# A later Q block ahead of the first Wo, and weight loads limited to two or three under way, in a transformer block on one core

## The chip, the cores and the metric

The kernel runs on one core of a Trainium2 chip. The metric is the device time of one execution in microseconds (us), as the median of several runs. The engines are TensorE (PE; its weight loads are listed as PEld), VectorE (DVE), ScalarE (ACT), GpSimd (POOL) and SyncE (SP), which issues every DMA of this kernel.

## The reference

One pre-norm transformer block over 2048 tokens of width 1024, in bf16, with 32 heads of 32 and an FFN width of 3584:

```python
def _A_ref(x, wqkv, wo):
    qkv = (x @ wqkv).reshape(B, S, 3, H, Dh) -> q, k, v   # H = 32, Dh = 32
    p = softmax(q @ k.T * Dh ** -0.5)                     # full attention, no mask
    return concat_heads(p @ v) @ wo
def _B_ref(x, w1, b1, w2, b2):
    return gelu(x @ w1 + b1) @ w2 + b2                    # tanh form of gelu
h   = x + _A_ref(layernorm(x), wqkv, wo)
out = h + _B_ref(layernorm(h), w1, b1, w2, b2)
```

The block above is cut and put in short form; `_layernorm` has no weights, and `B_x` is not used.

## The kernel before

The program is first recorded as a graph of tasks and then put into an order for each engine by a planner written in the kernel (`Graph.schedule`). Each task has an engine, a list of instructions, a planned duration and a priority; dependencies come from the buffers that it reads and writes (`Graph.add`), also where two buffers overlap in SBUF. The planner walks through planned time and, for each engine, picks among the ready tasks the one with the lowest priority number and, among equals, the one recorded first. For TensorE `pick_pe` chooses: scores (`qk`) always first, then the products with V (`pv`) and the row sums (`den`) when enough rounds wait, and otherwise the background (`bg`): projections, Wo and FFN. The order is then fixed: every engine runs its own list, and semaphore waits are put where a task depends on another engine. SyncE's DMAs go round 24 semaphores ("lanes"), and a DMA waits for the one before it on its lane. Planned DMA time counts 280 GB/s.

Attention is cut into jobs `(qb, g)`: 256 queries (`qb` from 0 to 7) and a group of 4 heads (`g` from 0 to 7). A job has 8 rounds of 256 keys; a round is 8 score matmuls (L796, four heads side by side), two exps of 128x1024 on ScalarE (L807), then 8 matmuls with V (L833), and row sums (L862) over sums made on VectorE (L848). When a job ends, VectorE normalises it into `OT` (L893).

The stages are these. At the start x is normalised, transposed into `xnT` (four blocks of 512 tokens) and K, V and Q for group 0 are computed while the first jobs run. Then for g from 1 to 7 `rest_of_projections(g)` computes K of group g, part of V, and Q of the first 512 tokens, beside the jobs of `qb` 0 and 1 (and of `qb` 2 for g in `EXTRA`). Q of the second 512 tokens is computed there for groups 0, 1 and 2 only. The normalised and transposed x of token blocks 1 to 3 is stored to DRAM (`xd`, shown as x_scratch), since the SBUF under `xnT` and the QKV weights (`Wall`) is used again by the FFN's buffers. `late_q(qc, half, gs)` later loads a block of x back into `xq`, loads the Q weights again in blocks of 256 columns, and computes the missing Q, which goes to DRAM (`qd`, shown as q_scratch) and comes back job by job in `load_q`.

After that come, for each 256 tokens `u`: `wo(u)` (attention output times Wo plus x, into `hch`), `ln2(u)` (layer norm; on all but the last `u` a DMA transpose into `hnT`), `ffn1(u)` (14 blocks of W1, bias on VectorE, gelu by tanh on ScalarE, L1014), and `ffn2(u, j)` (two column halves, 7 blocks of W2 each, two token tiles per half). They are background work beside the jobs of `qb = u + 3`, and the last of them (from `wo(7)` on) run alone at the end. Helper lines: L556 and L559 are background matmuls as four 32-column parts and as a whole, L562 those of the tail, L580 every plain DMA, L585 the DMA transpose.

Weights come from DRAM in blocks of 512 KB, into rings: four slots for W1 (`a_w1r`) and seven for W2 (`a_w2r`). Wo's two halves of 1 MB (`wov`) take two W1 slots each, and the weight blocks of `late_q` are also taken from the W1 ring. For the last `u` there are rings over the former K and V (`b_w1r`, `b_w2r`). A load waits until the slot's last reader is done. W1, W2 and Wo loads have priority 1, the transposes and Q loads -1, output stores 0. Where the recorded order matters most:

```python
    block_copies()
    late_q(1, 1, [g for g in range(2, G) if g not in EXTRA])
    wo(0)
    ln2(0)
    late_q(2, 0, range(G))
    late_q(3, 1, range(G))
    ffn1(0)
```

Of the kernel before, what the change touches and what calls it, by code (L numbers as in the profile page):

```python
# [10 lines left out]
E = mybir.EngineType  # L11

P = 128
BF = dt.bfloat16
F32 = dt.float32


# [43 lines left out]
class Graph:  # L61
# [47 lines left out]
    def schedule(self, pick_pe, pool, switch=0.104, dma_rate=280.0, dma_lat=2.1, dma_issue=0.06):  # L109
# [10 lines left out]
        events = []  # L120
        n = 0
        num = {t: i for i, t in enumerate(self.tasks)}

# [17 lines left out]
        while n < total:  # L141
# [5 lines left out]
            for e in self.ENGS:  # L147
                while free[e] <= now + 1e-9:
# [6 lines left out]
                    if e == E.PE:  # L155
                        t = pick_pe(rd, now, state, free_banks(now))
                    else:
                        t = min(rd, key=lambda x: (x.prio, num[x]))
                        if up and t.prio > 0:

                            for (rt, _, u) in up[:6]:
                                if u.prio < t.prio and rt < now + 0.6 * t.occ:
                                    t = None
                                    break
# [14 lines left out]
                    seqs[e].append(t)  # L179
                    if e == E.SP:  # L180
                        k = min(range(self.n_lanes), key=lambda i: lanes[i].done if lanes[i] else 0.0)
                        if lanes[k] is not None:
                            t.deps.add(lanes[k])
                            start = max(start, lanes[k].done)
                        lanes[k] = t
                        t.lane = k
                        free[e] = start + dma_issue
                        s0 = max(state["dma"], start + 0.9)
                        state["dma"] = s0 + t.bytes / dma_rate / 1e3
                        t.done = max(state["dma"], s0) + dma_lat - 0.9  # L190
                    else:
                        free[e] = start + t.occ
                        t.done = start + t.occ + t.lat
# [135 lines left out]
def build_kernel(nc, A_x, A_wqkv, A_wo, B_w1, B_b1, B_w2, B_b2, out):  # L329
# [6 lines left out]
    G = D // P  # L336
# [82 lines left out]

    xnT, B_xnTt = sb(ph0, "xnT", [P, 4, DC, 512], BF, 4, 4)  # L420
    k_hi = Area(B_KT[8 * (G - 2)].lo)
    Wall, B_W = [], []
    for k in range(6):
        h, b = sb(k_hi if k == 2 else ph0, "Wall%d" % k, [P, DC, 512], BF, 1, 4)
        Wall.append(h)
        B_W.append(b)
    assert k_hi.cur <= B_V[0].lo
# [228 lines left out]
    def tr_tile(tt, bank, evac, prio=0):  # L656
        tc, t4 = divmod(tt, 4)
        transposes(xb[:, tt % NXB, :], B_xb[tt % NXB], bank, xnT[:, tc, :, t4 * P:(t4 + 1) * P], B_xnTt[tc][t4], evac, prio)

    def proj(which, g, tc, bank, evac, direct=False):  # L660
# [4 lines left out]
        for dc in range(DC):  # L665
            mm(bank, Wall[blk][:, dc, c:c + P], xnT[:, tc, dc, :], dc == 0, dc == DC - 1,
               [B_W[blk][c // P]] + B_xnTt[tc], True, after=free if dc == 0 else ())
# [54 lines left out]
    def proj_v(tt, q, bank, evac, after=()):  # L722
# [3 lines left out]
        for k in range(2):  # L726
            tc, t4 = divmod(tt + k, 4)
            for dc in range(DC):
                mm(bank, xnT[:, tc, dc, t4 * P:(t4 + 1) * P], Wall[blk][:, dc, c:c + 256], dc == 0, dc == DC - 1,
                   B_W[blk][c // P:c // P + 2] + [B_xnTt[tc][t4]], True, cols=(256 * k, 256 * k + 256), after=after)  # L730
# [6 lines left out]
    def proj_v1(tt, g, n, bank, evac, c0=0, narrow=False, after=()):  # L737

        for k in range(n):
            tc, t4 = divmod(tt + k, 4)  # L740
            for dc in range(DC):
                mm(bank, xnT[:, tc, dc, t4 * P:(t4 + 1) * P], Wall[4][:, dc, P * g:P * g + P], dc == 0, dc == DC - 1,
                   [B_W[4][g], B_xnTt[tc][t4]], narrow, cols=(c0 + P * k, c0 + P * k + P), after=after)
# [11 lines left out]
    def proj_half(which, hc, bank, evac):  # L755
# [3 lines left out]
        for dc in range(DC):  # L759
            mm(bank, Wall[blk][:, dc, 0:P], xnT[:, tc, dc, 256 * h:256 * h + 256], dc == 0, dc == DC - 1,  # L760
               [B_W[blk][0]] + B_xnTt[tc][2 * h:2 * h + 2], True, cols=(0, 256))
# [256 lines left out]
    def ffn2(u, j, wide=False, W=None, banks=None):  # L1018
# [4 lines left out]
        for q in range(FC // 4):  # L1023
            s = W.next("w2", W.nw2)
            dma(W.w2[:, s, :, :], w2d[j, q], P * 4096, reads=[B_w2d[j][q]], writes=[W.B_w2[s]], prio=1)
            ws.append(s)
# [36 lines left out]
    def lead_norm(hc):  # L1063
# [6 lines left out]
        for tt in tts:  # L1070
            if tt < LEAD_PE:
                tr_tile(tt, slot(), "act" if tt in LEAD_ACT else "dve")
            else:
                tc, t4 = divmod(tt, 4)
                last_t[:] = [dma_transpose(xnT[:, tc, :, t4 * P:(t4 + 1) * P], xb[:, tt % NXB, :], P * 2048, [B_xb[tt % NXB]], [B_xnTt[tc][t4]], -4)]
            if tt + 8 < NT:
# [33 lines left out]
    lx = last_t or last_x[-1:]  # L1110
    for tc in range(1, 4):
        dma(xd[tc - 1], xnT[:, tc, :, :], P * 8192, reads=B_xnTt[tc], writes=[B_xd[tc - 1]], prio=1)
    rest_w(WK, 2 * P, 3 * P)
# [39 lines left out]
    for g in range(1, G):  # L1153
# [5 lines left out]
        if g in EXTRA:  # L1159
            attention(2, [g])  # L1160
    for g in range(1, 2):
        if g not in EXTRA:
            proj(0, g, 1, slot(), "dve")
    block_copies()
    late_q(1, 1, [g for g in range(2, G) if g not in EXTRA])
    wo(0)
    ln2(0)
    late_q(2, 0, range(G))
    late_q(3, 1, range(G))
# [147 lines left out]
```

## Time and profile before

| | us |
|---|---|
| median of 3 runs | 1081.65 (1079.47 to 1082.18) |
| the profiled execution | 1080.46 |
| its span, first to last instruction | 1078.7 |
| TensorE matmul busy | 1041.8 (97%) |
| ScalarE busy | 1012.8 (94%) |
| VectorE busy | 751.5 (70%) |
| exps (L807), 1024 of them, busy | 924.5 + 31.3 |
| mean granted TensorE clock | 0.994 |
| DMA | 196.37 MB, mean 182 GB/s |

The durations of all matmuls are modelled at their ends and overlap, so a busy TensorE is not a TensorE at its peak. An instruction's mean duration is longer than its share of a full engine: 1024-wide exps last 1.116 us each and overlap. The granted clock is the TensorE clock that the throttle let through. In the lists of a timeline the bracket at the end of a line is the idle time of the engine before it and what ended it; what is named there is the one that came last by the profile among several that were waited for.

### The profile page before, as it was taken

The numbers are of one execution on the slowest core, as the hardware profiler recorded it, in microseconds if no ns is written. First come the engines' busy times: TensorE is split into PE (matmuls) and PEld (weight loads), VectorE is DVE, ScalarE is ACT, GpSimd is POOL, SyncE is SP. The second block draws the span as 40 slices with busy tenths as digits, with TensorE's granted clock in tenths as the row PEclk, the third lists the DMA queues.
The fourth block names the chain that finished last, engine by engine and source line by source line (L and its number), as shares of the span: only waits on it lengthen the run. The fifth ranks groups of instructions, "written<-read, shape, count | busy, mean of one in ns | idle before, by whom it ended". The sixth has DMA issues, their size and how long they took to land.

```text
span 1078.7 us, 41723 instructions
## 1 busy us (share of the span) xinstructions
PE 1041.8 (97%) x18987; PEld 608.7 (56%) x19044; DVE 751.5 (70%) x1438; ACT 1012.8 (94%) x1116; POOL 43.4 (4%) x110
## 2 busy tenths in 40 slices
PE   8999999998899999999999999999999999899998
PEld 6566555554344754674475457447545744474483
DVE  8766666566586896698499669849966967596401
ACT  4999999999999999999999999999999999999650
POOL 4200000000010001001000100100010001000100
PEclk9999999999899999999999999999999999899999
DMA  8560544438474645744764574476466455866260
GB/s 233 151 184 21 154 137 119 139 119 296 157 188 134 206 172 181 251 167 154 260 221 168 188 247 165 149 258 221 158 210 233 178 192 206 241 230 238 91 242 20
DMA packets 136177, 196.37 MB, mean 182 GB/s; under 512 B 49216, under 2 KB 100288, under 8 KB 133184
## 3 DMA queue, kind: packets, MB, share of 16 engines
q1 hardware_dynamic: 136000, 193.70, 53.8%
q8 instruction: 149, 2.44, 0.9%
q14 instruction: 28, 0.23, 0.1%
HBM read 177.94 MB, written 27.26 MB: 190 GB/s over the span
## 4 chain that ended last, share of the span: by engine, by line
ACT 74%; PE 24%; DVE 2%; issue 1%; POOL 0%; POOLq 0%
ACT PT L807 67%; PE ps L559 6%; PE ps L562 5%; PE ps L556 5%; ACT uu L1014 4%; PE ps L796 3%; ACT PX L807 3%; PE ps L833 2%; PE ps L862 1%; PE ps L1055 1%; DVE PS L848 0%; PE ps L629 0%; ACT xnT L636 0%; DVE hch L957 0%; DVE st L608 0%
## 5 line engine op out<-in xcount | busy, mean ns | idle before, releaser
L807 ACT ACTIVATE PT<-ps 128x1024 bf16<-128x1024 f32 x992 | 924.5, 1116 | 7.4 <-PE ps L796 7.3
L848 DVE TENSOR_TENSOR PS<-PT 128x1024 bf16<-128x1024 bf16 x431 | 286.8, 686 | 125.8 <-ACT PT L807 65.1
L796 PE MATMUL ps<-QT,KT 32*128 32x256 bf16 x4096 | 205.0, 274 | 8.9 <-ACT PT L807 5.7
L833 PE MATMUL ps<-PT,V 128*32 128x256 bf16 x3968 | 175.7, 274 | 3.6 <-ACT PT L807 3.5
L796 PEld LDWEIGHTS ps<-QT,KT 32*128 32x128 bf16 x4096 | 61.0, 92 | 164.6 <-ACT PT L807 145.3
L862 PE MATMUL ps<-PS,ones 128*32 128x256 bf16 x1756 | 122.2, 274 | 3.0 <-DVE PS L848 2.7
L559 PE MATMUL ps<-hnT,a_w1r 128*128 128x256 bf16 x979 | 119.1, 273 | 1.7 <-DVE hch L1037 0.5
L833 PEld LDWEIGHTS ps<-PT,V 128*32 128x32 bf16 x3968 | 101.6, 97 | 33.4 <-ACT PT L807 6.3
L559 PEld LDWEIGHTS ps<-hnT,a_w1r 128*128 128x128 bf16 x979 | 90.1, 98 | 26.7 <-issue 15.7
L556 PE MATMUL ps<-a_w2r,gT 128*32 128x512 bf16 x1380 | 99.8, 381 | 0.4 <-DVE gT L1016 0.3
L559 PE MATMUL ps<-a_w2r,gT 128*128 128x512 bf16 x390 | 96.2, 380 | 2.8 <-issue 1.9
L556 PE MATMUL ps<-hnT,a_w1r 128*32 128x256 bf16 x2356 | 83.4, 276 | 1.4 <-DVE gT L992 1.0
L992 DVE TENSOR_TENSOR gT<-ps,b1f 128x512 bf16<-128x512 f32 x98 | 67.3, 687 | 14.5 <-PE ps L559 8.0
L1037 DVE SCALAR_TENSOR_TENSOR hch<-ps,hch 128x512 bf16<-128x512 f32 x32 | 22.0, 689 | 72.1 <-PE ps L562 47.1
L556 PEld LDWEIGHTS ps<-hnT,a_w1r 128*32 128x32 bf16 x2356 | 58.5, 97 | 15.2 <-issue 11.7
L559 PEld LDWEIGHTS ps<-a_w2r,gT 128*128 128x128 bf16 x411 | 35.3, 98 | 46.9 <-issue 12.5
L862 PEld LDWEIGHTS ps<-PS,ones 128*32 128x32 bf16 x1756 | 46.3, 96 | 25.1 <-DVE PS L848 8.8
L1014 ACT ACTIVATE uu<-uu 128x1024 bf16<-128x1024 bf16 x49 | 57.2, 1168 | 0.0
L559 PE MATMUL ps<-xnT,Wall 128*128 128x512 bf16 (+1 forms) x256 | 54.0, 344 | 2.4 <-issue 1.0
L556 PEld LDWEIGHTS ps<-a_w2r,gT 128*32 128x32 bf16 x1380 | 29.9, 96 | 25.7 <-issue 15.2
L613 POOL CAST mvb<-mv 128x2 bf16<-128x2 f32 (+1 forms) x25 | 5.1, 211 | 976.4 <-DVE mv L610 976.4
L878 DVE STREAM_TRANSPOSE OD<-ps 128x256 f32<-128x256 f32 x64 | 28.6, 447 | 11.5 <-PE ps L833 5.9
(91 smaller groups left out, 1018.4 us busy)
## 6 DMA issues: line engine op xcount, KB each, us to landing
a_w2r<-w_blocks SPq DMA_DIRECT2D x105, 512.0 KB, 5.6
a_w1r<-w_blocks SPq DMA_DIRECT2D x98, 512.0 KB, 3.7
wov<-wo_blocks SPq DMA_DIRECT2D x16, 1024.0 KB, 4.8
w_blocks<-in_B_w_dram SPq DMA_DIRECT2D x28, 512.0 KB, 4.0
b_w1r<-w_blocks SPq DMA_DIRECT2D x14, 512.0 KB, 4.1
a_w1r<-in_A_wqkv_dram SPq DMA_DIRECT2D x11, 512.0 KB, 5.2
Wall<-in_A_wqkv_dram SPq DMA_DIRECT2D x17, 256.0 KB, 4.5
xrb<-in_A_x_dram SPq DMA_DIRECT2D x16, 256.0 KB, 4.7
```

The lines of the kernel that those rows point to most:

```text
L556: fns.append(lambda p, j=j: p.matmul(psum[32 * j:32 * j + 32, bi(bank), c0:c1], lhsT[:, 32 * j:32 * j + 32], rhs, start=start, stop=stop, ...
L559: t.whole = lambda p: p.matmul(psum[:, bi(bank), c0:c1], lhsT, rhs, start=start, stop=stop, skip_group_check=True)
L562: t = pe(lambda p: p.matmul(psum[:, bi(bank), c0:c1], lhsT, rhs, start=start, stop=stop), occ, reads=reads, writes=[bb(bank)], mode="full" ...
L796: return p.matmul(psum[:, 2 * us[h // 2] + h % 2, 256 * i:256 * i + 256], KT[32 * h:32 * h + 32, g, k0:k0 + P], QT[32 * h:32 * h + 32, qs, :],
L807: act(lambda a, u=u, k=k: a.activation(PTs[s][:, k, :, :], psum[:, 2 * u:2 * u + 2, :], ACT.Exp, bias=0.0, scale=SCALE), 1024, reads=[B_ps ...
L833: fns.append(lambda p, i=i, h=h: p.matmul(psum[32 * h:32 * h + 32, bi(bank), 0:256], V[:, g, 2 * r + i, 32 * h:32 * h + 32], PTs[s][:, h / ...
L848: dve(lambda v: v.tensor_tensor(PS[:, n, :, :], pairs[:, :, 0:256], pairs[:, :, 256:512], ALU.add), c_dve(1024, 2), reads=B_PTs[s], writes ...
L862: fns.append(lambda p, h=h, rhs=rhs, i=i: p.matmul(psum[32 * h:32 * h + 32, bi(bank), 256:512], ones32[:, :], rhs, start=False, stop=last, ...
L878: t = dve(lambda v: v.transpose(OD[:, o, 1, :], psum[:, bi(bank), 256:512]), 0.36, reads=[self.B_O, self.B_D], writes=B_D, prio=-1)
L992: t = dve(lambda v: v.tensor_tensor(g[:, fc:fc + 2, :], psum[:, bi(bank), :].rearrange("p (f c) -> p f c", f=2), b1f[:, fc:fc + 2].unsquee ...
L1014: act(lambda a: a.activation(w, w, ACT.Tanh, bias=0.0, scale=KT2), 1024, reads=[B_uu[i]], writes=[B_uu[i]], prio=-1)
L1037: drop(dve(lambda v, hs=hs, bank=bank, half=half: v.scalar_tensor_tensor(hch[:, hs, c], psum[:, bi(bank), :], half, hch[:, hs, c], ALU.mul ...
```

## The change

The change has four parts.

1. The SBUF under `xnT` and `Wall` is laid out anew, so that the second block of x (`xnT1`) and the Q weights (`Wall0`, `Wall1`) lie under buffers that are needed late or not at once. Q of the second 512 tokens is then computed for groups 3 to 7 from `xnT1` and `Wall`, as it was for group 1 and 2. `late_q(1, ...)` is gone, and with it the store of that block of x. Other buffers lie elsewhere as a result: `hch` over `xnT1`, `xq` over `Wall4` and `xnT0`, the W1 ring over `xnT2`, `xnT3` and `Wall3`, the W2 ring over `Wall3`, `Wall5`, `Wall0` and `Wall1`.
2. `late_q(2, ...)` is recorded ahead of `wo(0)` and `ln2(0)`.
3. W2 loads get priority 2 and so yield to W1 and Wo loads.
4. Loads of 512 KB or more of priorities 1 and 2 are counted in units of 512 KB. The planner lets one go only when it makes at most three units (priority 1) or two (priority 2) under way, and adds a dependency on the completion of the load that has to be finished first. These loads are planned at 350 GB/s.

```diff
+BULK = {1: 3, 2: 2}
+UNIT = 1 << 19
...
+        def behind(t):
+            k = BULK[t.prio] - t.bytes // UNIT
+            for b in reversed(bulk):
+                k -= b.bytes // UNIT
+                if k < 0:
+                    return b
+            return None
...
-                        t = min(rd, key=lambda x: (x.prio, num[x]))
+                        go = rd
+                        if e == E.SP:
+                            go = []
+                            for x in rd:
+                                b = behind(x) if x.bytes >= UNIT and x.prio in BULK else None
+                                if b is None or b.done <= now + 1e-9:
+                                    go.append(x)
+                                else:
+                                    heapq.heappush(events, b.done)
+                            if not go:
+                                break
+                        t = min(go, key=lambda x: (x.prio, num[x]))
...
                     if e == E.SP:
+                        if t.bytes >= UNIT and t.prio in BULK:
+                            b = behind(t)
+                            if b is not None:
+                                t.deps.add(b)
+                            bulk.append(t)
...
-                        state["dma"] = s0 + t.bytes / dma_rate / 1e3
+                        state["dma"] = s0 + t.bytes / (350.0 if t.bytes >= UNIT and t.prio in BULK else dma_rate) / 1e3
...
-    xnT, B_xnTt = sb(ph0, "xnT", [P, 4, DC, 512], BF, 4, 4)
...
+    Wall[2], B_W[2] = sb(k_hi, "Wall2", [P, DC, 512], BF, 1, 4)
+    for kind, k in (("x", 1), ("W", 4), ("x", 0), ("x", 2), ("x", 3), ("W", 3), ("W", 5), ("W", 0), ("W", 1)):
+        h, b = sb(ph0, ("xnT%d" if kind == "x" else "Wall%d") % k, [P, DC, 512], BF, 1, 4)
...
-            dma(W.w2[:, s, :, :], w2d[j, q], P * 4096, reads=[B_w2d[j][q]], writes=[W.B_w2[s]], prio=1)
+            dma(W.w2[:, s, :, :], w2d[j, q], P * 4096, reads=[B_w2d[j][q]], writes=[W.B_w2[s]], prio=2)
...
-    for tc in range(1, 4):
-        dma(xd[tc - 1], xnT[:, tc, :, :], P * 8192, reads=B_xnTt[tc], writes=[B_xd[tc - 1]], prio=1)
+    for tc in range(2, 4):
+        dma(xd[tc - 1], xnT[tc][:, :, :], P * 8192, reads=B_xnTt[tc], writes=[B_xd[tc - 1]], prio=1)
...
-    for g in range(1, 2):
-        if g not in EXTRA:
-            proj(0, g, 1, slot(), "dve")
+    for g in range(3, G):
+        proj(0, g, 1, slot(), "dve")
     block_copies()
-    late_q(1, 1, [g for g in range(2, G) if g not in EXTRA])
+    late_q(2, 0, range(G))
     wo(0)
     ln2(0)
-    late_q(2, 0, range(G))
     late_q(3, 1, range(G))
```

More of the change, by code (lines that the diff above doesn't have):

```diff
@@ L121, in schedule @@
         n = 0
+        bulk = []
+        def behind(t):
[5 more added lines that the diff above has]
+            return None
         num = {t: i for i, t in enumerate(self.tasks)}
@@ L417, in build_kernel @@
     ffn = Area(top.cur)
-    xnT, B_xnTt = sb(ph0, "xnT", [P, 4, DC, 512], BF, 4, 4)
     k_hi = Area(B_KT[8 * (G - 2)].lo)
[L422 to L426, printed above, removed]
+    Wall, B_W = [None] * 6, [None] * 6
+    xnT, B_xnTt = [None] * 4, [None] * 4
+    Wall[2], B_W[2] = sb(k_hi, "Wall2", [P, DC, 512], BF, 1, 4)
+    for kind, k in (("x", 1), ("W", 4), ("x", 0), ("x", 2), ("x", 3), ("W", 3), ("W", 5), ("W", 0), ("W", 1)):
+        h, b = sb(ph0, ("xnT%d" if kind == "x" else "Wall%d") % k, [P, DC, 512], BF, 1, 4)
+        if kind == "x":
+            xnT[k], B_xnTt[k] = h, b
+        else:
+            Wall[k], B_W[k] = h, b
     assert k_hi.cur <= B_V[0].lo
@@ L657, in tr_tile @@
         tc, t4 = divmod(tt, 4)
-        transposes(xb[:, tt % NXB, :], B_xb[tt % NXB], bank, xnT[:, tc, :, t4 * P:(t4 + 1) * P], B_xnTt[tc][t4], evac, prio)
+        transposes(xb[:, tt % NXB, :], B_xb[tt % NXB], bank, xnT[tc][:, :, t4 * P:(t4 + 1) * P], B_xnTt[tc][t4], evac, prio)
     def proj(which, g, tc, bank, evac, direct=False):
@@ L665, in proj @@
         for dc in range(DC):
-            mm(bank, Wall[blk][:, dc, c:c + P], xnT[:, tc, dc, :], dc == 0, dc == DC - 1,
+            mm(bank, Wall[blk][:, dc, c:c + P], xnT[tc][:, dc, :], dc == 0, dc == DC - 1,
                [B_W[blk][c // P]] + B_xnTt[tc], True, after=free if dc == 0 else ())
@@ L728, in proj_v @@
             for dc in range(DC):
-                mm(bank, xnT[:, tc, dc, t4 * P:(t4 + 1) * P], Wall[blk][:, dc, c:c + 256], dc == 0, dc == DC - 1,
+                mm(bank, xnT[tc][:, dc, t4 * P:(t4 + 1) * P], Wall[blk][:, dc, c:c + 256], dc == 0, dc == DC - 1,
                    B_W[blk][c // P:c // P + 2] + [B_xnTt[tc][t4]], True, cols=(256 * k, 256 * k + 256), after=after)
@@ L741, in proj_v1 @@
             for dc in range(DC):
-                mm(bank, xnT[:, tc, dc, t4 * P:(t4 + 1) * P], Wall[4][:, dc, P * g:P * g + P], dc == 0, dc == DC - 1,
+                mm(bank, xnT[tc][:, dc, t4 * P:(t4 + 1) * P], Wall[4][:, dc, P * g:P * g + P], dc == 0, dc == DC - 1,
                    [B_W[4][g], B_xnTt[tc][t4]], narrow, cols=(c0 + P * k, c0 + P * k + P), after=after)
@@ L759, in proj_half @@
         for dc in range(DC):
-            mm(bank, Wall[blk][:, dc, 0:P], xnT[:, tc, dc, 256 * h:256 * h + 256], dc == 0, dc == DC - 1,
+            mm(bank, Wall[blk][:, dc, 0:P], xnT[tc][:, dc, 256 * h:256 * h + 256], dc == 0, dc == DC - 1,
                [B_W[blk][0]] + B_xnTt[tc][2 * h:2 * h + 2], True, cols=(0, 256))
@@ L1074, in lead_norm @@
                 tc, t4 = divmod(tt, 4)
-                last_t[:] = [dma_transpose(xnT[:, tc, :, t4 * P:(t4 + 1) * P], xb[:, tt % NXB, :], P * 2048, [B_xb[tt % NXB]], [B_xnTt[tc][t4]], -4)]
+                last_t[:] = [dma_transpose(xnT[tc][:, :, t4 * P:(t4 + 1) * P], xb[:, tt % NXB, :], P * 2048, [B_xb[tt % NXB]], [B_xnTt[tc][t4]], -4)]
             if tt + 8 < NT:
```

## The prediction

> **What bounds the kernel now.** I read the busy shares first, then the windows by engine, then ScalarE's own timeline for its gaps, then SyncE's timeline.
>
> ```profile
> PE 1041.8 (97%) x18987; PEld 608.7 (56%) x19044; DVE 751.5 (70%) x1438; ACT 1012.8 (94%) x1116; POOL 43.4 (4%) x110
> ACT  4999999999999999999999999999999999999650
> PEclk9999999999899999999999999999999999899999
> ```
>
> ScalarE (ACT) is full in 36 of 40 slices, and the clock row dips twice, near 290 and near 930 us. ScalarE's 1024 exps and 49 tanhs run back to back: the chain of waits has 178 exps in 163.48 us, 0.918 us each, so 1073 of them are 985.5 us. The first starts at 22.28 and the last ends at 980.76 + 31.43 = 1012.2. That leaves about 4.3 us of gaps, and ScalarE's timeline lists nearly all of them:
>
> ```profile
> 292.21 11.12 ACT L807 ACTIVATE PT<-ps 128x1024 bf16<-128x1024 f32 x12 [1.55 <-PE ps L796]
> 303.52 16.89 ACT L807 ACTIVATE PT<-ps 128x1024 bf16<-128x1024 f32 x18 [0.19 <-PE ps L796]
> 646.20 2.86 ACT L807 ACTIVATE PT<-ps 128x1024 bf16<-128x1024 f32 x3 [0.47 <-PE ps L796]
> 729.20 8.36 ACT L807 ACTIVATE PT<-ps 128x1024 bf16<-128x1024 f32 x9 [0.22 <-PE ps L796]
> 917.41 14.83 ACT L807 ACTIVATE PT<-ps 128x1024 bf16<-128x1024 f32 x16 [0.37 <-PE ps L796]
> 933.74 8.36 ACT L807 ACTIVATE PT<-ps 128x1024 bf16<-128x1024 f32 x9 [1.50 <-PE ps L796]
> ```
>
> The bracket is the idle time before the group: 1.74 us around 290 to 303, 1.87 us around 917 to 933, 0.69 us elsewhere. After 1012.2 comes a tail of 66.5 us of plain matmuls. So the change can win at most 4.3 us (0.4%) before the tail, and it has to win it in those places. The windows show why they are there (busy us of each engine in each stretch, then granted clock, DMA share, GB/s):
>
> ```profile
> 259.00:266.70 7.70, 5.00 (x105) 1.97 (x108) 4.03 (x7) 7.63 (x10) 0.00 (x0) 1.00 0.95 347
> 281.60:289.00 7.40, 4.37 (x80) 1.59 (x78) 4.26 (x11) 7.40 (x9) 0.00 (x0) 0.73 0.82 288
> 289.00:303.50 14.50, 14.31 (x227) 6.52 (x228) 9.95 (x20) 12.78 (x14) 2.23 (x4) 0.90 0.41 97
> 917.00:930.20 13.20, 9.09 (x182) 3.45 (x183) 7.24 (x13) 12.83 (x15) 0.00 (x0) 0.87 1.08 277
> 930.20:935.00 4.80, 4.54 (x100) 2.75 (x96) 1.07 (x3) 3.30 (x5) 0.00 (x0) 0.65 0.16 61
> ```
>
> Three times TensorE (first pair) runs out of background work (projections, Wo, FFN) and only serves attention. ScalarE stays full meanwhile. In the second and third stretch the granted clock then falls to 0.50 (in 2 us windows, 286 to 290 and 928 to 932), and ScalarE loses its time just afterwards, when background work is back and TensorE still runs at half clock. The first stretch is starved as long, but keeps its clock and costs nothing.
>
> **The change part by part.** Sums are against the profiled execution: 1080.46 us, its span of 1078.7 plus 1.76 around it. The median of the runs, 1081.65, lies 1.2 above it.
>
> *Q of the second 512 tokens from resident x.* Gone are one 1 MB store, one 1 MB load and three 512 KB weight loads (11 of that row become 8). The 5 x 8 matmuls stay, with the same 512 columns. The stretch 259 to 266.7 was the wait for that load of x (issued around 251 to 256) and its weight block; TensorE gets about 2.7 us of background time back there. ScalarE lost nothing in it: value 0.
>
> *The later Q block ahead of the first Wo.* At 281.6 TensorE had finished the old late Q, and wo(0) had to wait for attention head group 7: its OT is written at 288.14 + 0.41 and wo(0) starts at 289.02. late_q(2) stood behind wo(0) because its weight blocks take ring slots that Wo's weights hold. In the changed program's order it comes first: 64 matmuls x 0.22 us (24 in 5.3 us in the tail) = 14 us of TensorE work in front of a hole where 7.40 - 4.37 = 3.0 us are free. Counting the background matmuls between one round of scores and the next, the order of before has six rounds without any in this neighbourhood (two, then four in a row), the new one has one, and that is full of attention work. So I take the first clock drop as gone: -1.55 - 0.19 = -1.74. Two prices. wo(0) comes later by the 14 us of work; the background of the attention phase ends at 1004.2 (last ffn2(6,0) matmul) against the last exp at 1012.2, which is 8 us of cover, and the refilled 5.7 us go into it. If that cover were gone, each us would cost one. And the first block of late_q(2) can load only when the last V matmul has released the x under its ring slot; 16 projection matmuls (3 rounds, 5.5 us) stand in between, and such loads land in 5.2 us (median). Bound 0 to 1.5; I take 0.3, since the median just fits.
>
> *Buffers in another order.* The w2 ring now lies under weight blocks that the late Q projections still read, so its early loads wait for them; they are first read at 401, over 100 us later. The x rows for Wo (hch) wait for the last projection from the second x block; they land in 4.5 us, and late_q(2) covers them. 0 for both.
>
> *Two or three weight loads under way, w2 behind w1.* SyncE issues in order, so a wait for a load holds up everything queued behind it: Q loads (needed many rounds later), output stores, and the two DMA transposes of hnT that FFN1 needs. Before, the queue looked like this ahead of the last starved stretch:
>
> ```profile
> 904.46 2.96 SPq L580 DMA_DIRECT2D a_w1r<-w_blocks  x4
> 907.92 3.35 SPq L580 DMA_DIRECT2D a_w2r<-w_blocks  x4
> 911.31 3.60 SPq L585 DMA_TRANSPOSE hnT<-a_xb  x1
> 915.01 1.04 SPq L580 DMA_DIRECT2D b_w1r<-w_blocks  x1
> 916.09 0.43 SPq L580 DMA_DIRECT2D a_w2r<-w_blocks  x1
> 916.56 2.80 SPq L585 DMA_TRANSPOSE hnT<-a_xb  x1
> ```
>
> Ten blocks, 5.2 MB, are ahead of the second transpose; at the 390 GB/s of those windows that is 13 us, and the transposes' landing spreads from 2.7 to 8.9 us. With at most 1.5 MB under way the backlog is 4 us, so the transpose gains up to 6. But the order takes this back: before, half of ffn2(5,1) lay between the end of wo(6) (906.4) and the hole (918.3), 11.9 us of cover for layer norm and transposes. In the new order ffn2(5,1) is done first and three of the four tiles of wo(6) are the last background work. The chain behind them is exposed: 8.1 us from the last add to a_xb (907.32 to 915.45), about 1 for the add, 1.3 to issue and 2.8 to 6.8 to land, 13 to 17 us, against a hole of 11.9 before. The order shows six rounds without background there in both programs. So I keep the second drop: 0, with bounds -1.87 (no drop) and +1.9 (a longer stay at half clock, once more the same loss).
>
> Supply under the limit: a load lands in 3.9 us (median of a_w1r) and takes 0.35 to issue, so two under way bring a block every 2.1 us, three every 1.4. A pass of ffn2 over one token tile reads a block per four matmuls, 0.88 us of TensorE, about 1.5 us beside attention. Over the six later blocks two under way fall 3.6 us behind, unless the first lies ready that much earlier. Slots are released one by one in the pass before, some 10 us ahead, so I take 0; bound 3.6 for a pass. [...] In the tail the last b_w1r load is issued at 1010 for a stage that starts at 1027, and a_w2r and b_w2r over 20 us ahead: 0.
>
> Sum: 1080.46 - 1.74 + 0.3 = 1079.0 as a profiled execution, and 1.2 more as a median: **1080.2**.
>
> **The rivals.**
> *Both clock drops go* (0.2). For it: the transposes lose their backlog, and equally starved stretches have not always dropped the clock (259 to 266.7). Against it: six rounds without background in the new order. 1081.65 - 1.74 - 1.87 + 0.3 = 1078.3. [...]
> *Nothing is gained* (0.2). The drop at 290 comes elsewhere, for example where wo(0) waits for its second half of weights (1 MB, landing 4.6 to 10.2 us, loadable only when late_q(2) has left the slots). For it: two rounds near there have a single background matmul. 1081.65.
> *Slower: w2 starves ffn2* (0.1). Place: the first pass of ffn2 in the five stages u = 1 to 5, where w2 now yields to w1 and waits two deep. If the first block is ready less than 3.6 us ahead, TensorE, which runs in order, stops with the next scores behind the stopped matmul. Half the shortfall, 1.8 us less 0.3 in hand, five times is 7.5 us: 1080.2 + 7.5 = 1087.7. Against it: SyncE's loads never show as TensorE waits in the trace of before.
>
> **How the numbers follow.** The forecast, one drop gone and one kept, gets 0.5. The measurement tells about 0.3% (3.2 us) from no change; the three runs spread over 2.7. Faster by more needs less than 1078.4: half of the both-drops case and the lower end of the forecast, 0.17. Slower by more needs over 1084.9: the w2 case and a little, 0.11. Between them 0.72. The range goes from 1077.6 (both drops and the small gaps) to 1083.2 (no gain, and the 1.5 us of the first block).
>
> **What would show it.** Right: clock 1.00 from 259 to 303, no ScalarE gap over 0.3 us there, a hole without background just before ffn1(6) at some 910 to 925 with clock 0.50 behind it and 1.5 to 2 us of ScalarE gaps, the last exp at about 1010.7, the same tail of 66.5 us. Wrong: a full clock throughout (then both drops), a drop between 285 and 310 (no gain), or ScalarE gaps that repeat every 94 us at the start of ffn2 (starved w2).

## The result, and the profile after

The changed kernel takes 1090.44 us (median of 6 runs, 1087.05 to 1091.86), the kernel before 1080.82 us on the same chip (6 runs). The ratio is 1.0087, 95% interval 1.0069 to 1.0104: slower by 0.9%, where 1080.2 us was forecast, a change too small to measure. The profiled execution took 1091.77 us with a span of 1089.8, against 1080.46 and 1078.7.

The page of the changed kernel, the lines that answer to those of before (busy time and share by engine, the rows of slices, and the shares of the chain of waits):

```profile
PE 1052.4 (97%) x18834; PEld 607.8 (56%) x18834; DVE 749.7 (69%) x1438; ACT 1014.9 (93%) x1116; POOL 44.1 (4%) x110
ACT  4999999999999999999999999999999999899650
PEclk9999999999999999999999999999999999899899
ACT 50%; PE 31%; DMA 13%; DVE 5%; issue 1%; POOL 1%; SPq 1%; POOLq 0%; DVEq 0%
```

The first dip of the clock row, near 290 us, is gone, and there is a new one shortly before the tail. In the chain DMA has 13%; before, the same row had none:

```profile
ACT 74%; PE 24%; DVE 2%; issue 1%; POOL 0%; POOLq 0%
```

ScalarE's timeline of the changed kernel shows where it stood still; the bracket is the idle time ahead of a group:

```profile
450.50 1.02 ACT L840 ACTIVATE PT<-ps 128x1024 bf16<-128x1024 f32 x1 [0.58 <-PE ps L829]
486.91 29.61 ACT L840 ACTIVATE PT<-ps 128x1024 bf16<-128x1024 f32 x32 [0.95 <-PE ps L829]
517.42 26.73 ACT L840 ACTIVATE PT<-ps 128x1024 bf16<-128x1024 f32 x29 [0.90 <-PE ps L829]
...
668.39 4.69 ACT L840 ACTIVATE PT<-ps 128x1024 bf16<-128x1024 f32 x5 [0.99 <-PE ps L829]
...
811.41 14.93 ACT L840 ACTIVATE PT<-ps 128x1024 bf16<-128x1024 f32 x16 [0.85 <-PE ps L829]
...
935.95 1.94 ACT L840 ACTIVATE PT<-ps 128x1024 bf16<-128x1024 f32 x2 [2.27 <-PE ps L829]
939.10 9.27 ACT L840 ACTIVATE PT<-ps 128x1024 bf16<-128x1024 f32 x10 [1.21 <-PE ps L829]
...
1012.15 9.32 ACT L840 ACTIVATE PT<-ps 128x1024 bf16<-128x1024 f32 x10 [0.79 <-PE ps L829]
1024.71 0.39 ACT L915 ACTIVATE OD<-ps 128x256 f32<-128x256 f32 x1 [3.24 <-DVE OD L911]
```

All listed gaps up to the last exp make 11.56 us, against 4.30 before. To see what each came from one asks TensorE's timeline just ahead of it. TensorE waits of 0.15 us or longer that a DMA ended did not exist before. There are 11 now, 7.5 us in all: ten for weight loads (6.2 us) and one for the transpose into hnT. Four of them:

```profile
483.34 1.90 PE L592 MATMUL ps<-wov,OT 128*128 128x512 bf16 x8 [1.03 <-DMA wov<-wo_blocks]
516.00 1.04 PE L592 MATMUL ps<-a_w2r,gT 128*128 128x512 bf16 x4 [0.82 <-DMA a_w2r<-w_blocks]
809.65 0.61 PE L589 MATMUL ps<-a_w2r,gT 128*32 128x512 bf16 x8 [0.81 <-DMA a_w2r<-w_blocks]
933.88 1.47 PE L589 MATMUL ps<-hnT,a_w1r 128*32 128x256 bf16 x24 [1.36 <-DMA hnT<-a_xb]
```

ScalarE's gaps at 486.91, 517.42, 811.41 and 935.95 stand right behind them. The chain of waits around the second of these, and SyncE's timeline (issue time, time to issue, DMAs in a row) show the limit at work:

```profile
507.02 4.54 DMA a_w2r<-w_blocks
...
511.58 4.37 DMA a_w2r<-w_blocks
...
516.00 1.04 PE ps L592 x4
```

```profile
501.72 0.32 SPq L613 DMA_DIRECT2D a_w2r<-w_blocks  x1
503.51 0.32 SPq L613 DMA_DIRECT2D QT<-q_scratch  x1
503.87 0.43 SPq L613 DMA_DIRECT2D a_w2r<-w_blocks  x1
505.74 1.24 SPq L618 DMA_TRANSPOSE hnT<-a_xb  x1
507.02 1.24 SPq L613 DMA_DIRECT2D a_w2r<-w_blocks  x2
510.58 0.34 SPq L613 DMA_DIRECT2D out_dram<-hch  x1
511.58 4.71 SPq L613 DMA_DIRECT2D a_w2r<-w_blocks  x3
```

These are the seven W2 blocks of the second pass of ffn2 in this stage (the second column half). They go out over 14.6 us. Four of them, the one at 501.72 and the last three, start when an earlier load has just landed; the transpose of hnT stands in the same queue. TensorE reads the first four blocks between 510.69 and 515.18:

```profile
510.69 1.67 PE L592 MATMUL ps<-a_w2r,gT 128*128 128x512 bf16 x7 [0.17 <-DVE hch L1070]
...
512.63 1.47 PE L592 MATMUL ps<-a_w2r,gT 128*128 128x512 bf16 x6
...
514.36 0.82 PE L592 MATMUL ps<-a_w2r,gT 128*128 128x512 bf16 x3
```

The fifth, which it reads at 516.00, was issued at 511.58, when one that was issued at 507.02 had landed. In the kernel before, the seven blocks of the same pass went out within 6.1 us (509.71 to 515.84):

```profile
509.71 6.13 SPq L580 DMA_DIRECT2D a_w2r<-w_blocks  x7
```

Set against its first matmul, each block of a second pass was issued 7 to 11 us ahead in the kernel before (second trace, e9 below) and landed 1.8 us or more ahead. In the changed kernel the lead falls within each such pass from 7 to 9 us to about 4, and one block or more lands only as it is read. Up to the tail the blocks of the first passes are issued over 45 us ahead in both kernels.

The windows of the changed kernel (busy us of PE, PEld, DVE, ACT, POOL, then granted clock, DMA share, GB/s) give the clock:

```profile
281.60:289.00 7.40, 7.11 (x128) 3.35 (x118) 5.74 (x12) 7.40 (x9) 0.00 (x0) 1.00 0.75 244
921.00:928.00 7.00, 4.01 (x80) 1.64 (x72) 5.54 (x15) 6.74 (x8) 2.43 (x4) 0.78 1.02 239
928.00:940.00 12.00, 8.98 (x188) 4.84 (x188) 4.31 (x7) 8.44 (x9) 0.00 (x0) 0.70 0.66 178
1014.00:1020.00 6.00, 4.15 (x68) 1.21 (x68) 2.46 (x4) 6.00 (x8) 0.00 (x0) 0.75 0.01 3
```

The hole at 281.6 is filled and keeps its clock. The hole ahead of ffn1(6) is still there. Ahead of the tail the last background matmul ends 9.7 us before the last exp, 8.0 before the change, and the clock now drops there as well: the tail's first ScalarE step waits 3.24 us instead of 1.44, and the tail takes 68.3 us instead of 66.5.

The whole difference of the spans, by term:

| term | us |
|---|---|
| first clock drop gone (1.55 + 0.19) | -1.7 |
| nine ScalarE gaps behind waits for loads of W1, W2, Wo | +5.5 |
| gaps around ffn1(6), 3.82 instead of 1.87 | +1.9 |
| other listed gaps, 2.2 instead of 0.7 (1.5 of it, at 668 and 827, behind TensorE stops without a cause, for which see below) | +1.5 |
| the rest of the stretch from the first continuous exps to the last, without a gap of 0.15 us or longer (999.8 - 11.56 against 989.9 - 4.30) | +2.6 |
| tail | +1.8 |
| start of the exps, 21.67 instead of 22.28 | -0.6 |
| sum (measured 11.1) | 11.0 |

### The profile page after: what moved, and what is told of

It reads as the page before. It is cut to its first block, busy times and chain, and to the rows that moved or that the text cites. A ratio compares the mean times of both kernels' runs of the same rounds, so it can differ in the third digit from the quotient of the medians.

```text
span 1089.8 us, 41382 instructions
## 1 busy us (share of the span) xinstructions
PE 1052.4 (97%) x18834; PEld 607.8 (56%) x18834; DVE 749.7 (69%) x1438; ACT 1014.9 (93%) x1116; POOL 44.1 (4%) x110
## 4 chain that ended last, share of the span: by engine, by line
ACT 50%; PE 31%; DMA 13%; DVE 5%; issue 1%; POOL 1%; SPq 1%; POOLq 0%; DVEq 0%
ACT PT L840 45%; PE ps L592 11%; DMA a_w2r<-w_blocks 9%; PE ps L589 6%; PE ps L595 5%; PE ps L829 4%; PE ps L866 3%; ACT PX L840 3%; DMA a_w1r<-w_blocks 2%; ACT uu L1047 2%; PE ps L895 2%; DVE PS L881 1%; DVE gT L1025 1%; DVE st L641 1%; DMA wov<-wo_blocks 1%
## 5 line engine op out<-in xcount | busy, mean ns | idle before, releaser
L592 PE MATMUL ps<-hnT,a_w1r 128*128 128x256 bf16 x938 | 114.9, 273 | 1.8 <-DMA a_w1r<-w_blocks 1.2
L589 PE MATMUL ps<-a_w2r,gT 128*32 128x512 bf16 x1416 | 103.3, 382 | 1.2 <-DMA a_w2r<-w_blocks 1.0
L592 PE MATMUL ps<-a_w2r,gT 128*128 128x512 bf16 x402 | 99.8, 380 | 4.5 <-DMA a_w2r<-w_blocks 2.8
L592 PEld LDWEIGHTS ps<-hnT,a_w1r 128*128 128x128 bf16 x938 | 86.1, 98 | 26.3 <-issue 14.7
L589 PE MATMUL ps<-hnT,a_w1r 128*32 128x256 bf16 x2520 | 94.0, 277 | 5.6 <-DVE gT L1025 3.1
L589 PEld LDWEIGHTS ps<-hnT,a_w1r 128*32 128x32 bf16 x2520 | 62.6, 97 | 22.5 <-issue 15.7
L592 PE MATMUL ps<-xnT,Wall 128*128 128x512 bf16 (+1 forms) x335 | 73.2, 353 | 0.5 <-ACT xnT L669 0.2
L1047 ACT ACTIVATE uu<-uu 128x1024 bf16<-128x1024 bf16 x49 | 52.8, 1078 | 0.2 <-DVE uu L1046 0.2
L592 PE MATMUL ps<-wov,OT 128*128 128x512 bf16 x187 | 46.7, 381 | 2.6 <-DMA wov<-wo_blocks 1.0
L592 PEld LDWEIGHTS ps<-xnT,Wall 128*128 128x128 bf16 x335 | 28.7, 98 | 30.7 <-issue 9.3
```

The costliest lines, as they stand in the source:

```text
L589: fns.append(lambda p, j=j: p.matmul(psum[32 * j:32 * j + 32, bi(bank), c0:c1], lhsT[:, 32 * j:32 * j + 32], rhs, start=start, stop=stop, ...
L592: t.whole = lambda p: p.matmul(psum[:, bi(bank), c0:c1], lhsT, rhs, start=start, stop=stop, skip_group_check=True)
L1047: act(lambda a: a.activation(w, w, ACT.Tanh, bias=0.0, scale=KT2), 1024, reads=[B_uu[i]], writes=[B_uu[i]], prio=-1)
```

## The experiments

The runs came in five sets, each on one chip with the kernel before beside it; there the kernel before took 1084 to 1086 us and spread from 1079 to 1091, wider than in the first comparison. Ratios are to the kernel before of the same set, with their 95% intervals.

### Parts of the change

The order of parts 1 and 2 alone, in the changed kernel:

```diff
-BULK = {1: 3, 2: 2}
+BULK = {}
...
-            dma(W.w2[:, s, :, :], ..., prio=2)
+            dma(W.w2[:, s, :, :], ..., prio=1)
```

> The changed kernel without its third and fourth part: no limit on loads under way, W2 loads back at priority 1, all loads planned at 280 GB/s; the new buffer layout, the resident Q and the later Q block ahead of wo(0) stay. Theory (the waits for finished loads make W2 late and TensorE stops in order): the loss is gone and the gain of the filled hole shows, 1079 to 1080 us, ScalarE gaps of about 4 us or less up to the last exp, clock 1.00 from 280 to 300. Rival A (the new order with its tighter planned loads is what is late, waits or not): the order is planned anew at 280 here, so also 1079 to 1081. Rival B (the new layout or the moved Q block costs the time, for example by later first loads into the W2 ring): it stays at 1088 to 1091.

Measured: 1090.62 us, 1.0057 [1.0030, 1.0083]. Parts 3 and 4 alone, put into the kernel before:

```diff
+BULK = {1: 3, 2: 2}
...
+                            b = behind(t)
+                            if b is not None:
+                                t.deps.add(b)
...
-            dma(W.w2[:, s, :, :], ..., prio=1)
+            dma(W.w2[:, s, :, :], ..., prio=2)
```

> The kernel before with only the third and fourth part: three or two loads under way, W2 at priority 2, these loads planned at 350 GB/s; old layout, old late Q. Theory (waits make W2 late): about the whole loss plus the hole that is not filled, 1090 to 1093 us, SyncE waiting some 100 us for loads, TensorE waits ended by W2 loads. Rival A (planned order): the same, 1090 to 1093. Rival B (layout): no loss, 1080 to 1082.

Measured: 1098.47 us, 1.0115 [1.0073, 1.0158]. The changed kernel in its own planned order, but with no wait added for it:

```diff
-                            b = behind(t)
-                            if b is not None:
-                                t.deps.add(b)
```

> The changed kernel with the planned order of every engine kept as it is, but without the waits for a finished load that the limit adds (a load still waits for its slot's readers and its lane). Theory (waits): loads go out up to some us earlier, W2 is on time, 1079 to 1081 us. Rival A (the order itself is too tight, since it was planned with loads at 350 GB/s and W2 behind W1): the loss stays, 1087 to 1091. This run tells the two apart.

Measured: 1089.38 us, 1.0039 [1.0020, 1.0058]. The changed kernel with a wider limit:

```diff
-BULK = {1: 3, 2: 2}
+BULK = {1: 6, 2: 6}
```

> The changed kernel with six units under way for both priorities instead of three and two. Theory (a chain of two leaves the DMA engines empty between loads): with six under way they stay full, most of the loss goes, 1080 to 1083 us, and SyncE waits for loads fall from 108 us to under 40. Rival A (planned order at 350 GB/s): the order is still planned at 350, so 1086 to 1090.

Measured: 1091.62 us, 1.0061 [1.0037, 1.0086]. The expectations were for a kernel before of 1080.8 us; it took 1085.5 here. Less these 4.7 us, e1 (1086.0) and e3 (1084.7) lie between theory and rival, e2 (1093.8) just over the theory's range, and e4 (1087.0) in that of its rival A, so the theory alone does not hold. By the medians the limit alone, in the order of before, costs the most, though its interval touches that of e1. Without the limit's waits (e3) six W2 loads still came late, 3.5 us in all, so the order that was planned for the limit costs something too. And parts 1 and 2, which were to gain 1.7 us, lose 0.6% by themselves. In that kernel no load ends a TensorE wait. TensorE's timeline has instead stops without a cause, four of them over 1 us, one in each of four stages and in the middle of runs of equal matmuls:

```profile
536.67 0.72 PE L589 MATMUL ps<-hnT,a_w1r 128*32 128x256 bf16 x18 [1.31 <-issue]
...
635.23 0.29 PE L829 MATMUL ps<-QT,KT 32*128 32x256 bf16 x4 [1.20 <-issue]
...
729.92 0.38 PE L866 MATMUL ps<-PT,V 128*32 128x256 bf16 x5 [1.26 <-issue]
...
828.52 1.27 PE L589 MATMUL ps<-hnT,a_w1r 128*32 128x256 bf16 x38 [1.48 <-issue]
```

In the five kernels the two kinds of loss trade places (TensorE waits of 0.15 us or longer between 24 and 1031 us):

| kernel | ended by a DMA, us | stops without a cause, us |
|---|---|---|
| changed | 7.5 | 1.3 |
| e1, no limit | 0 | 6.8 |
| e2, limit alone | 6.7 | 5.5 |
| e3, order only | 3.5 | 2.1 |
| e4, six under way | 1.0, none for W1, W2 or Wo | 5.0 |

### What the stops are

The queue of instructions (q8) moved 148 packets of 16 KB in this kernel, and TensorE has 37,776 matmuls and weight loads: 255 to a packet, which fits TensorE's program being fetched. The DMA queues of that kernel in the 12.3 us ahead of the first of those stops (packets, MB, share of 16 engines), first from 521.9 to 534.2, with the DMA engines' busy tenths in 40 slices:

```profile
DMA  0000000290009399939597888999999989989999
...
q1 hardware_dynamic: 978, 2.94, 69.5%
q14 instruction: 1, 0.01, 0.2%
```

and from 534.2 to 535.4:

```profile
q1 hardware_dynamic: 111, 0.41, 96.5%
q8 instruction: 1, 0.02, 4.9%
```

No packet of TensorE's program came for 12 us; from about 527 on the bulk loads filled the engines (DMA share 0.99 from 528 to 536). One came at 534.3, and TensorE, which had stopped at 535.4, went on at 536.7. The packet records say the same of all seven fetches of this kernel that came 390 or more instructions after the one before (the median is about 250): they came 2.3 to 3.3 us after TensorE had begun 256 instructions, and behind each of them TensorE stopped, for 0.24 to 1.48 us, and went on 2.2 to 2.4 us after the packet had begun. The other traces agree: of the 50 stops of 0.5 us or more in all 20 of them, 48 end 2.1 to 2.7 us after such a packet began. While a packet that came 390 or more instructions after the last was awaited, the DMA engines were busy at 0.98 (median of 93); ahead of those on time, at 0.46. Only 37 of the 93 have a stop of 0.5 us or more behind them. A 4 KB packet of a weight load takes 0.159 us, so 2.3 to 3.3 us are the time of 14 to 21 of them, an estimate; what a late fetch waits behind on the DMA engines was not shown.

So theory F: a fetch that falls due while bulk loads fill the engines comes late, and what it costs depends on where in the program it falls. Two kernels with TensorE's instructions shifted against the fetches, and the changed kernel once more beside them:

```diff
-    for k in range(80):
-        pe(lambda p: p.matmul(psum[:, 6, 0:256], ident[:, :], b2t[:, 0:256], start=True, stop=True), ...)
+    for k in range(78):
+        one = lambda p: p.matmul(psum[:, 6, 0:256], ident[:, :], b2t[:, 0:256], start=True, stop=True)
+        small = lambda p: p.matmul(psum[0:32, 6, 0:8], ident[:, 0:32], b2t[:, 0:8], start=True, stop=True)
+        pe([small] * 8 if k < 10 else one, ...)
```

> The changed kernel as it is, so that the other variants and it stand on one chip beside the kernel before. Theory: slower than before by 9 to 10 us (0.8 to 0.95%), as in the result, whatever the level of the chip.

Measured: 1096.90 us, 1.0109 [1.0065, 1.0154]. Its trace has waits of 10.8 us for weight loads (those for W2 all in second passes again), 1.0 us for hnT, and 2.7 us of stops.

> The changed kernel without the limit (as in e1), with TensorE's instruction stream moved by about 130 instructions: ten of the first warm-up matmuls become eight tiny ones each and two are left out. Nothing later changes. Theory F (without the limit TensorE runs out of instructions once a stage, because their fetch queues behind a burst of W2 loads, and where in the stream that falls decides the price): the four stops of 1.2 to 1.5 us at 537, 635, 730 and 829 us move, shrink or go; the sum of TensorE waits without a named cause changes by 2 us or more from e1's 6.8. Rival G (these stops have a fixed cause in the program, a certain wait or bank): they stay where they are, 1.2 to 1.5 us each, and the time is e1's.

Measured: 1094.18 us, 1.0102 [1.0064, 1.0141].

> The kernel before with the same move of TensorE's instruction stream by about 130 instructions. Theory F: the kernel before owes its time in part to a lucky place; stops of about 1 us appear in some stages where it had none over 0.6, and it becomes 2 to 6 us slower. Rival G: within 1.5 us of the kernel before (up to 1.5 us from a later start may be in it).

Measured: 1089.57 us, 1.0050 [1.0029, 1.0071]. The shift made both orders slower and moved the stops without removing them: parts 1 and 2 shifted have 7.2 us of them, at 446, 544, 639, 738 and 836 among others. They also have a clock drop again near the place of the first, 0.50 from 303.0 to 306.4: TensorE waited 2.35 us there for a staging buffer of late_q(2), whose store to DRAM had taken 7.6 us, and ScalarE lost 2.73 and 0.57 us. The stops of e6 fit theory F. e7 doesn't show it: the kernel before became slower too, but its stops stayed small in the profiled run (2.6 us).

One more run asks what a clock drop costs, by matmuls without a use in both holes of the kernel before:

```diff
+    def fill(n, after):
+        for k in range(n):
+            bank = slot()
+            t = pe(lambda p, bank=bank: p.matmul(psum[:, bi(bank), 0:512], ident[:, :], hold_x[:, 0:512], start=True, stop=True), 0.216,
+                   reads=[B_ident, B_b2t], writes=[bb(bank)], kind="warm", after=[after])
...
+    fill(20, hole1)
...
+        if u == 5:
+            fill(28, hole2)
```

> The kernel before with 48 extra matmuls whose results nobody reads, 20 for the hole without background work at 281 to 289 us and 28 for that at 917 to 930. Theory (the holes cost only by the clock drop behind them): granted clock 1.00 through both places, ScalarE's gaps of 1.74 and 1.87 us gone, 3 to 3.6 us faster than before. Rival H (the gaps come from the work that returns late, not from the clock): clock full but gaps of 1 us or more stay, within 1 us of before.

Measured: 1084.53 us, 0.9999 [0.9977, 1.0022]. The clock stayed at 1.00 and both gaps went, but four stops of 0.75 to 1.71 us had come in at 553, 648, 747 and 840, which fits the 48 instructions having shifted the program too. The run decides nothing about the clock.

### With fewer bytes

If bulk loads are behind both losses, kernels that load less must lose neither. In three kernels the W1 and W2 loads keep their place, their planned time and their waits, but bring a quarter of a block:

```diff
+            n = 1 if (W, 2, s) in filled else 4
+            filled.add((W, 2, s))
-            dma(W.w2[:, s, :, :], w2d[j, q], ...)
+            dma(W.w2[:, s, 0:n, :], w2d[j, q][:, 0:n, :], ...)
```

> The kernel before, unchanged, for its trace on the chip of the experiments, where it runs at 1085.5 instead of 1080.8 us. Ratio 1.000 within 0.002. Theory F (a late instruction fetch stops TensorE when bulk loads fill the DMA engines, and how long depends on where in the program the fetch falls): TensorE's stops without a cause, 0.15 us or longer, sum to about 6 us as in the first trace, none much over 1 us. Rival C (this chip's memory is slower for everything): several stops of 1.2 to 1.7 us here too, summing to 8 us or more, so that the stops of the other kernels on this chip would be no effect of their order.

Measured: 1084.53 us, 0.9992 [0.9965, 1.0019]. The profiled run was one of its slower ones (1088.92 us), and TensorE's timeline has stops that the first trace of the same kernel does not have:

```profile
957.23 0.75 PE L556 MATMUL ps<-hnT,a_w1r 128*32 128x256 bf16 x18 [1.33 <-issue]
974.62 1.93 PE L556 MATMUL ps<-hnT,a_w1r 128*32 128x256 bf16 x64 [1.76 <-issue]
```

Rival C is half right: the stops (7.8 us in all) are no property of the new order. They come and go between runs of one program. The 6 us that the expectation gives the first trace are mostly not stops: 29 gaps of 0.16 us stand where a matmul's record is missing (19,044 weight loads, 18,987 matmuls), and three stops of 1.4 us in all are left.

> The kernel after, in the same order and with the same waits, but most loads of W1 and W2 blocks bring only a quarter of the block (the rest of the slot keeps older weights, so the result is another): about 7 instead of 16 MB per stage. Theory L (what the change costs is the bulk loads: load waits of TensorE, 7.5 us, and late instruction fetches): both vanish, TensorE's DMA waits under 1 us, and the time is 1078 to 1084 where before is 1085.5. Rival W (the waits cost by what they hold up in SyncE's queue, not by how long a load takes): still 1088 or more. Rival O (the new order itself costs): 1085 to 1090, the same as the next kernel and over the last one.

Measured: 1079.45 us, 0.9949 [0.9930, 0.9968].

> Parts 1 and 2 of the change alone (no limit on loads), with quarter loads as in the kernel ahead of it. Theory L: no stop of TensorE over 0.6 us without a cause, where the same order with whole loads had four of 1.2 to 1.5 us; the time is 1078 to 1083, at most 1 us above and up to 3 us below the next kernel, by the first clock drop that is gone. Rival O (the order of parts 1 and 2 costs some 5 us by itself): 4 to 6 us above the next kernel.

Measured: 1081.88 us, 0.9974 [0.9959, 0.9989].

> The kernel before with quarter loads in the same way. Theory L: its small stops (6 us of 0.16 to 1 us) go for the most part, both clock drops stay: 1080 to 1084 on this chip. Rival C: no gain, 1085 to 1086.

Measured: 1081.45 us, 0.9967 [0.9949, 0.9986]. With a quarter of the bytes the changed kernel, waits and order kept, is the fastest of the three by the medians, though the intervals overlap. Rivals W and O fall: with short loads neither the waits nor the order cost anything. (A shorter load also ends sooner what is held behind it in the queue: a quarter block of W2 landed in 2.6 us in e10, a whole one in 4.4 us in the changed kernel. The run does not tell these two apart.) Between 24 and 1031 us no load ends a TensorE wait of 0.15 us or longer in any of the three traces, the stops make 0.7, 1.6 and 0.2 us (one of 0.83 in the second, over the 0.6 that was expected), and the chain of the changed kernel is ScalarE's again:

```profile
ACT 83%; PE 13%; DVE 2%; POOL 1%; DMA 0%; issue 0%; SPq 0%; POOLq 0%; DVEq 0%
```

The runs also spread less: 1078.2 to 1080.9 and 1080.7 to 1083.0 for the two new orders.

Part of this can be had with the computation whole. The W2 ring holds one column half of W2. If a stage begins with the half that the stage before ended with, that half needs no loads (a_w2r: 63 loads instead of 105):

```diff
-        ws = []
-        for q in range(FC // 4):
+        ws = kept.get((W, j), [])
+        if not ws:
+            for q in range(FC // 4):
...
+        kept.clear()
+        kept[W, j] = ws
...
-        ffn2(u, 0)
+        ffn2(u, u % 2)
         ln2(u + 1)
-        ffn2(u, 1)
+        ffn2(u, 1 - u % 2)
```

> The kernel before, with the two column halves of ffn2 taken in turn (0,1 then 1,0): the half that comes last in a stage is still in the W2 ring when the next stage begins with it, and its seven blocks are not loaded again. Six times 7 of the loads of a_w2r go (3.7 MB each time), the result is the same. Theory L (bulk loads that fill the DMA engines delay the instruction fetch): the loads of W2 that were in flight with those of W1 at the start of ffn1 are gone, stops without a cause sum to under 3 us, and the time is 1081 to 1084 where before is 1084.7 on such a chip, with a smaller spread. Rival B (it is the bytes as a whole, so a fifth less saves little): 1084 to 1085.

Measured: 1082.37 us, 0.9978 [0.9955, 1.0000].

> The kernel after, limit included, with the halves of ffn2 in turn. Theory L, with the load waits in the first pass of ffn2, where the first blocks come too late: that pass needs no loads now, TensorE's load waits fall from some 7.5 us to under 4 (the second pass still loads two deep), time 1081 to 1086. Rival T (the waits come in the second pass, whose slots come free only while the pass before runs): the waits stay, 1089 or more.

Measured: 1090.56 us, 1.0064 [1.0044, 1.0084].

> Parts 1 and 2 alone, no limit, with the halves of ffn2 in turn. Theory L: the four stops of 1.2 to 1.5 us at the start of ffn1 are gone, no load wait comes in, time 1079 to 1083, the fastest of these four or equal to the first. Rival O (the order of parts 1 and 2 costs something besides the loads): 1085 or more, 3 us above the first of the four.

Measured: 1083.07 us, 0.9977 [0.9958, 0.9996].

> The kernel after in its planned order without the limit's waits, with the halves of ffn2 in turn. Theory L: between the second and the third of these four, 1080 to 1085; load waits under 2 us. Rival T: as the second, 1087 or more.

Measured: 1084.89 us, 1.0015 [0.9995, 1.0035]. Parts 1 and 2 go from 1.0057 to 0.9977, and their stops from 6.8 to 2.1 us: the loss of e1 went with the late fetches. These runs also price the limit where few stops hide it, on one chip and with intervals that do not touch: 1090.56 us with it against 1083.07 without is 7.5 us, and 5.7 of them go when only its waits are taken out (1084.89). With the limit the halves in turn gain little, and rival T holds: the loads of the first pass are gone, yet DMAs still end TensorE waits of 9.9 us, 8.2 of them for W2 and all of these in the second pass:

```profile
517.42 1.04 PE L592 MATMUL ps<-a_w2r,gT 128*128 128x512 bf16 x4 [0.81 <-DMA a_w2r<-w_blocks]
...
709.71 1.04 PE L592 MATMUL ps<-a_w2r,gT 128*128 128x512 bf16 x4 [1.02 <-DMA a_w2r<-w_blocks]
...
811.99 0.62 PE L589 MATMUL ps<-a_w2r,gT 128*32 128x512 bf16 x8 [0.62 <-DMA a_w2r<-w_blocks]
...
1013.01 1.04 PE L592 MATMUL ps<-a_w2r,gT 128*128 128x512 bf16 x4 [2.01 <-DMA a_w2r<-w_blocks]
```

Last, the clock drops again, now with few stops left to hide them: `fill` added to both orders; in the order of before with 20 matmuls in the first hole as well.

```diff
         ffn1(u + 1)
+        if u == 5:
+            fill(28, hole2)
...
     ffn2(6, 0)
+    fill(14, [last_bg()])
```

> Parts 1 and 2 with the halves of ffn2 in turn, and 42 plain matmuls more (28 in the hole ahead of ffn1(6), 14 after ffn2(6,0)) that keep TensorE busy where it has no background. Theory K (with the fetch stops mostly gone, a clock drop costs what its ScalarE gaps show): the granted clock stays at 1.00 to the tail, the gaps of the second drop (0.35 + 1.50 + 0.23 us in the kernel without the fill) and 1.5 us ahead of the tail go: 1079 to 1080.5, against 1083.1 without. Rival H (the filler only shifts the loss, as 48 of them did in the kernel before: 1084.5 against 1085.6): 1082 to 1084.

Measured: 1079.08 us (1078.01 to 1081.27), 0.9962 [0.9944, 0.9980].

> The kernel before with the halves of ffn2 in turn, and 62 plain matmuls more (20 in the hole ahead of the first Wo, 28 in the one ahead of ffn1(6), 14 after ffn2(6,0)). Theory K: the gaps of the first drop (1.61 + 0.66 + 0.28 us) and 1.5 us ahead of the tail go: 1078 to 1080, against 1082.4 without. Rival H: 1081.5 to 1083.

Measured: 1078.70 us (1077.18 to 1080.61), 0.9953 [0.9935, 0.9971]. Both lie where theory K put them, 4.0 and 3.7 us under the same kernels without the fill, though these ran on another chip (the kernel before took 1084.1 there and 1085.0 here) and the intervals of the ratios overlap. The granted clock is 1.000 over the span in both profiled runs, and ScalarE's timeline of the last kernel has only these gaps up to the tail:

```profile
341.86 16.81 ACT L807 ACTIVATE PT<-ps 128x1024 bf16<-128x1024 f32 x18 [0.31 <-PE ps L796]
358.99 9.55 ACT L807 ACTIVATE PT<-ps 128x1024 bf16<-128x1024 f32 x10 [0.33 <-PE ps L796]
374.31 3.77 ACT L807 ACTIVATE PT<-ps 128x1024 bf16<-128x1024 f32 x4 [0.22 <-PE ps L796]
663.07 4.74 ACT L807 ACTIVATE PT<-ps 128x1024 bf16<-128x1024 f32 x5 [0.86 <-PE ps L796]
1010.85 0.38 ACT L882 ACTIVATE OD<-ps 128x256 f32<-128x256 f32 x1 [1.43 <-DVE OD L878]
```

This kernel and the one before it are faster than the kernel before, and so than the changed one. The order of parts 1 and 2 makes no difference between them that these runs can tell.

## Why the prediction was wrong, step by step

*What bounds the kernel.* Right: ScalarE, with 4.3 us of gaps. That cap on the gain (0.4%, and the tail) is about what the last experiment reached (0.5%).

*Q of the second 512 tokens from resident x: 0.* Right for the two traces compared. TensorE is now busy for all of 259 to 266.7 (7.70 us instead of 5.00), and ScalarE lost nothing there before or after. In the second trace of the kernel before (e9) the clock did fall in this stretch, to 0.50 from 265.2 to 268.6, and ScalarE lost 0.37 and 0.51 us behind it, so the term is not always nothing.

*First clock drop gone: -1.74.* Right in place and size, but buried under the rest; in the shifted kernel e6 a drop came back at 303, where the rival "nothing is gained" had looked for one, but behind a store and not behind Wo's weights. The 0.3 us for the first block of late_q(2) was not needed; ScalarE has no gap of 0.15 us or longer before 450.

*8 us of cover behind the background, no price for more of it.* Wrong. The cover was counted in time to the last exp, but a hole there is one more hole, and the clock fell in it: 0.75 from 1014 to 1020, tail +1.8 us. That it is the longer cover (9.7 us) that did it is not shown: the clock fell there in four later traces in the order of before too (e2, e7, e12, e13).

*Second drop kept: 0, bounds -1.87 and +1.9.* The mechanism held, so the rival with both drops gone fell: wo(6) is the last background work and the transposes behind it are exposed (TensorE waits 1.36 us for hnT). The size was at the upper bound, +1.95.

*Two under way: 0, bound 3.6 for a pass.* This is the step that failed: the shortfall of a pass was set at less than half of what it is. The prediction had a block every 2.1 us and TensorE taking 1.5 us for one, 0.6 us lost at each. In the pass shown above the blocks went out 2.4 us apart (501.72 to 515.97), and TensorE took 1.1 us for one (510.69 to 515.18 for four), so 1.3 us were lost at each. The first block landed 5.8 us ahead of its read, more than the 3.6 that were asked for, and still the fifth landed as it was read. Before, slots came free one by one some 10 us ahead, as the prediction says. The limit spends that lead: it counts the loads of W1, W2 and Wo together, and a held load holds what stands behind it in SyncE's queue, which waited 108.0 us for W2 loads in the changed kernel and for no load of W1, W2 or Wo before. With the waits for W1 and Wo it cost 5.5 us of ScalarE gaps. The rival "w2 starves ffn2" (0.1; 1087.7 us) had the mechanism, but not the place: W1, Wo and hnT were waited for as well, and every W2 wait lies in the second pass of a stage, in the changed kernel and in the run with no loads in the first. With the limit alone (e2) the ratio is 1.0115.

*What no step had.* The prediction took loads that nobody waits for as free. They are not: while they fill the DMA engines (busy at 0.98) TensorE's own program comes late, in e1 seven times by 2.3 to 3.3 us. Parts 1 and 2 without the limit lost 0.6% with such stops. The limit does soften this (stops of 1.3 and 2.7 us in the two traces of the changed kernel, 6.8 without it), and pays more for it in load waits.

*Still open.* Why a stop comes at one place in one run and not in the next run of the same program. And the 2.6 us by which the exps took longer outside the listed gaps were not traced to a cause.

## What to carry to other kernels

Before putting a limit on loads, find the shortest time between the release of a slot and its first read, and take from it all that the limit and the issuing queue can hold up ahead of that load. Better than spreading loads is not to need them: going through the weights forth and back keeps what the ring holds, and with it most of the fetch stops went (6.8 to 2.1 us with parts 1 and 2), at no cost that these runs show. Look at every hole in the background, the last one before a tail too, and price it by the gaps behind it. Take more than one trace for that: the drops and the stops of one program were not the same in two of them.

## What the runs showed of the hardware that was not expected

- By the traces TensorE's program is loaded while it runs: a queue of instructions (q8), counted on the same 16 DMA engines as the weights, moved 148 packets of 16 KB in e1, one for some 255 of TensorE's instructions. With these 0.97 busy or so (96.5% in the window above), seven fetches of e1 came 2.3 to 3.3 us late, and over all runs TensorE stopped for up to 1.8 us (e9) without any wait in the profile but "issue".
- These stops differ between runs of one program: two traces of the kernel before have 1.4 and 7.8 us of them. It ran from 1079 to 1091 us in the five sets; with a quarter of most W1 and W2 blocks from 1079.6 to 1084.4.
- Equally starved stretches lower the granted clock in one run and not in another. Ahead of the tail, TensorE busy for 4.15 of 6.0 us went with 0.75 in the changed kernel, and 4.13 of 6.20 us with 1.00 in the kernel before; from 259 to 266.7 the kernel before kept 1.00 in its first trace, with 5.00 us busy, and had 0.90 in its second, with 5.42.
